# Attention and a squared-ReLU feed-forward on one core: the first batch's stores behind the third batch's transposes, and a smaller planned cost of exp

## The chip, the core and the metric

The kernel runs on one core of a Trainium2 chip. The metric is the time of one execution on the device in microseconds (us). Of the kernel before, four runs are given: median 421.77 us, from 421.56 to 421.96.

## What is computed

Grouped-query attention of 8 batches (16 query heads, 4 key and value heads, 384 positions, head size 64), followed by a feed-forward on the 3072 tokens:

```python
scores = q @ k.T / sqrt(64)            # each key head serves 4 query heads
attn   = exp(scores) / sum(exp(scores))
x      = (attn @ v)                     # heads side by side: [3072, 1024]
h      = maximum(x @ w_in, 0)           # [3072, 2048]
out    = (h * h) @ w_out                # [3072, 1024]
```

The reference subtracts the row's maximum before exp; the kernel does without, since the scores are small. Inputs and output are float32; the kernel multiplies in bf16 and adds up in float32.

## The kernel before, in words

**Stages.** The work goes by batch. For a batch b, SyncE's DMA transposes bring keys and queries into the layouts `kT` and `qT` (`turn_k_dma`, L277; `turn_q_dma`, L283, in two halves of eight heads each). For batch 0 and part of batch 1, TensorE transposes instead (L296, L313). Then:

- scores: `burst_small`, TensorE L339, writes pieces of two PSUM banks each, a total of 512 columns in each bank; ScalarE takes exp of a piece in one instruction (L349) into `expT`. Pieces alternate between banks 0, 1 and banks 2, 3, so that a piece needs the exp of the piece but one before it to be done. A batch has 18 pieces; the first half of the queries serves the first nine.
- values: `av`, TensorE L365, 8 steps of 18 matmuls in each batch; VectorE takes reciprocals of the row sums (L374) and multiplies (L380) into `o_sb`, which frees the bank of the step. SyncE transposes `o_sb` into `xT` (L385).
- feed-forward up: TensorE L460 in quads of four tiles (`quad`). A quad is 64 matmuls on half of the rows of the array each, in eight parts of eight, in banks 4 to 7; VectorE applies the maximum with zero (L473) and squares (L480, some on ScalarE, L477) into `h2T`. A batch has four quads; batch 0 computes four of its tiles with whole rows, early (L423).
- feed-forward down: TensorE L522, VectorE copies the sum to `y_sb` (L531), SyncE stores it (L534). There are six such copies and stores in a batch, and six halves of `y_sb`.

**What lies beside what.** The scores of batch b + 1 are issued between the quads of batch b, so that ScalarE's exp runs beside TensorE's feed-forward. The stretch with scores and quads is called split in the code. When it is over, the values of batch b + 1 follow, then the down products of batch b. GpSimd issues the loads of q, k and v two batches ahead and of both weight matrices, copies keys twice side by side (`dup_k`, L268), and copies values (`aug_v`, L273).

**What sets the order.** Each engine runs its own instructions in the order in which they are recorded (`Recorder.add`); semaphores carry the dependencies. The order comes from a planner, the loop from L666. It keeps a modelled clock for each engine (`R.clock`), advanced by the `cost` of each recorded operation, and models the time at which an operation's inputs and banks are free (`R.when`). At each turn it lists candidates (turn, values, scores "sc", feed-forward "ffn", ...) with their times, and takes the one of best priority among those that are ready. So a cost moves no work by itself; it decides in which order instructions stand on TensorE, and which wait comes with them. Two rules matter here. For the scores, L721 sets the time:

```python
t = max(R.when(reads=reads) + 3.0 * (b == 2 and not split), R.when(writes=[...]))
```

and for opening a split stretch, L735 and L736 ask for batches from 2 on that the planned time of the transposed queries lies within 6 us.

**Chores.** `prepare(b)` (L625) queues five steps: `dup_k`, the key transpose, the two halves of the query transpose, `aug_v`. Each is issued by the planner at L688 when its input is planned to be there. Stores are recorded at once, in `down_part`, when the last of the four parts of a down product is recorded. When all chores of a batch are issued, `turned` takes that batch's number.

Of the kernel before, what the change touches and what calls it, by code (L numbers as in the profile page):

```python
# [141 lines left out]
def bass_gqa_attention__then__ffn_squared_relu_kernel(  # L142
# [24 lines left out]
    R = Recorder(nc)  # L167
# [26 lines left out]
    def bank(i):  # L194
        return ps[:, i, :]
# [4 lines left out]
    def pick(allowed):  # L200
        turn_count[0] += 1
        i = min(allowed, key=lambda i: (max(R.when(writes=[("bank", i)]), R.clock["tensor"]), used[i]))
        used[i] = turn_count[0]
        return i
# [119 lines left out]
    def score_reads(b, u, c0=0, n=HC):  # L324
        g = u // NJ
        return [("kT", b % 2, g)] + [("qT", b % 2, g, t) for t in range(c0 // 128, (c0 + n) // 128)]

    def q_cols(b, g, x, c0, c1):
        flat = qT[b % 2][64 * x:64 * x + 64, 6 * g:6 * g + 6, :].rearrange("p n c -> p (n c)")
        return flat[:, c0:c1]  # L330

    def burst_small(b, pieces, base):

        n, c0, wide = (b * NU + pieces[0][0]) % NEX, pieces[0][1], pieces[0][2]

        def sc(pe):
            for m, (u, _, _) in enumerate(pieces):
                for x in range(2):
                    mm = pe.matmul(ps[:, base + x, m * wide:(m + 1) * wide],  # L339
                                   kT[b % 2][64 * x:64 * x + 64, u, :], q_cols(b, u // NJ, x, c0, c0 + wide))  # L340
            return mm

        total = wide * len(pieces)
        keys = [("bank", base), ("bank", base + 1)]
        R.add("tensor", sc, reads=[r for p in pieces for r in score_reads(b, *p)], writes=keys,
              cost=total / 2400 + (0.01 if b else 0.2))
        src = ps[:, base:base + 2, 0:total].rearrange("p x (k c) -> p x k c", k=len(pieces))
        dst = expT[:, n:n + len(pieces), :, c0:c0 + wide].rearrange("p k x c -> p x k c")
        R.add("scalar", lambda e: e.activation(dst, src, AF.Exp, scale=0.125), reads=keys,  # L349
              writes=[("expT", (b * NU + u) % NEX, t) for u, _, _ in pieces  # L350
                      for t in range(c0 // 128, (c0 + wide) // 128)], cost=(0.3 if b else 0.07) + total / 600)

    def av_reads(b, c):
        return [("expT", (b * NU + c // 2 * NJ + j) % NEX, 3 * (c % 2) + t) for j in range(NJ) for t in range(3)] + [("v_aug", b % 2), ("v_one", b % 2)]
# [138 lines left out]
    def downs(b):  # L493

        items = []
        for jj in range(2 if b == 0 else 0):
            ats = [[] for _ in range(NJ)]
            for tiles in ((0, 1), (2,)):
                for half in range(2):
                    for i3 in tiles:  # L500
                        for part in (2 * half, 2 * half + 1):
                            items.append(down_part(b, jj, i3, 512 * jj, 512 * jj + 512, part, ats[i3]))
        for jj in range(2 if b else 0):
            for i3 in range(NJ):
                last = b == B - 1 and (jj, i3) == (1, NJ - 1)
                for c0, c1 in ((512, 896), (896, 1024)) if last else ((512 * jj, 512 * jj + 512),):
                    at = []
                    for part in range(4):
                        items.append(down_part(b, jj, i3, c0, c1, part, at))
        return items  # L510

    def down_part(b, jj, i3, c0, c1, part, at):
        n = c1 - c0

        def piece():
            if part == 0:
                at.append(pick((6, 7)))
            i = at[0]

            def mm(pe):  # L520
                for c in range(4 * part, 4 * part + 4):
                    m = pe.matmul(bank(i)[:, 0:n], h2T[:, c, i3 * 128:(i3 + 1) * 128],  # L522
                                  w_out_sb[:, c, c0:c1], start=(c == 0), stop=(c == NFC - 1))
                return m

            R.add("tensor", mm, reads=need, writes=[("bank", i)], cost=4 * (n / 2400 + 0.0025))
            if part == 3:
                yb = y_n[0] % (2 * NY)
                y_n[0] += 1
                ysl = y_sb[yb // 2][:, (yb % 2) * 512:(yb % 2) * 512 + n]  # L530
                R.add("vector", lambda e: e.tensor_copy(ysl, bank(i)[:, 0:n]),  # L531
                      reads=[("bank", i)], writes=[("y", yb)], cost=0.08 + n / 960)
                rows = out[b * S:(b + 1) * S, :].rearrange("(p j) f -> j p f", j=NJ)[i3]
                R.add("sync", lambda e: e.dma_start(rows[:, c0:c1], ysl),  # L534
                      reads=[("y", yb)], writes=[("out", b, i3, c0)], dma=f"y{yb}", cost=0.6)
                stored.append(("out", b, i3, c0))

        need = [("w_out", jj, part // 2)] + [("h2T", c) for c in range(4 * part, 4 * part + 4)]
        return 0, need, (6, 7) if part == 0 else None, piece

    stored = []


    ones = nc.const_aps.tensor(1.0, (128, 128), bf16)
# [5 lines left out]
        out=ident[:], in_=ident[:], compare_op=ALU.not_equal, fill=1.0, base=0,  # L550
# [26 lines left out]
    def warm_up(n, cost):  # L577
        def body(pe):
# [8 lines left out]
          reads=[("k_f32", 0)], writes=[("k_dup", 0, 0, 0)], cost=0.27)  # L587
    R.add("scalar", lambda e: e.copy(k_dup[0][:, 0:NJ, 1, :], k_f32[:, 0:NJ, :]),
          reads=[("k_f32", 0)], writes=[("k_dup", 0, 0, 1)], cost=0.27)
# [3 lines left out]
          reads=[("q_f32", 0)], writes=["q_lead"], cost=0.3)  # L593
    for n in range(2):
        a, z = 384 * n + 192 * (n == 0), 384 * n + 384
        R.add("scalar", lambda e, a=a, z=z: e.copy(q_to[:, a:z], q_from[:, a:z]),
              reads=[("q_f32", n)], writes=[("q_st", 0, 0, n)], cost=0.35 + 0.15 * n)
# [17 lines left out]
    sc_q = [(b, n) for b in range(B) for n in range(len(later if b else smalls))]  # L615
# [3 lines left out]
    scored, pairs, turned = set(), 0, 1  # L619
# [13 lines left out]
    def open_bank(banks):  # L633
        return min(R.when(writes=[("bank", i)]) for i in banks)
# [3 lines left out]
    def ff_head(split):  # L638

        if ff["now"]:  # L640
            return ff["now"][0]
        n = 4 if split else 1
        if ff["tiles"]:
            if len(ff["tiles"]) < n:
                return None
            return (quad(ff["b"], ff["tiles"][:4]) if split else up_tile(ff["b"], ff["tiles"][0]))[0]
        return ff["down"][0] if ff["down"] and not split else None
# [14 lines left out]
    split = False  # L662
# [3 lines left out]
    while av_q or av_open or sc_q or o_q or lanes or ff["now"] or ff["tiles"] or ff["down"]:  # L666
        now = R.clock["tensor"]
# [20 lines left out]
        while chores and R.when(reads=chores[0][0], eng="none") <= now + margin:  # L688
            chores.pop(0)[1]()
            if not chores:  # L690
                turned = queued
        cand = []
        wait = 0.1 if split else 0.0
        if turn_q:
            b, g, w = turn_q[0]
# [5 lines left out]
        elif av_q:  # L701
            b, c = av_q[0]
# [6 lines left out]
        if sc_q:  # L709
            b, u = sc_q[0]  # L710
            pieces = (later if b else smalls)[u]
            tiles = {(b, x, t) for x, c0, n in pieces for t in range(c0 // 128, (c0 + n) // 128)}
            ok = {(b, x // NJ, t) for _, x, t in tiles} <= turned_g if b < 2 else turned >= b
            ok = ok and pairs // 2 * NJ + NEX > b * NU + max(x for _, x, _ in tiles)
            if b and not split:
                ok = ok and at_edge and (u > 0 or pairs >= 8 * b and ff["b"] == b - 1 and len(ff["tiles"]) >= 4)
            if ok:
                reads = [r for p in pieces for r in score_reads(b, *p)]
                if b and not split:
                    reads += [("xT", (b - 1) % NXT, kc) for kc in range(NKC)]  # L720
                t = max(R.when(reads=reads) + 3.0 * (b == 2 and not split), R.when(writes=[("bank", 2 * (u % 2) + i) for i in range(2)]))  # L721
                cand.append((t, 0, "sc"))
        early_banks[:] = [i for i in ((6, 7, 0, 1, 2, 3) if sc_q and sc_q[0] == (1, 0) else (6, 7)) if i not in held]
        for n, lane in enumerate(lanes):
            chunks, need, banks, _ = lane[0]
            if x_done[0] >= chunks:
                t = R.when(reads=need)
                if banks is not None:
                    if not banks:
                        continue  # L730
                    t = max(t, open_bank(banks))
                cand.append((t, 5 + 0.1 * n, n))
        opening = (not split and at_edge and bool(sc_q) and sc_q[0][1] == 0 and sc_q[0][0] == ff["b"] + 1
                   and pairs >= 8 * sc_q[0][0] and len(ff["tiles"]) >= 4)
        if opening and sc_q[0][0] > 1:  # L735
            opening = R.when(reads=score_reads(sc_q[0][0], 0)) < now + 6.0  # L736
        f_head = ff_head(split or opening) if not lanes else None
        if f_head is not None:
            chunks, need, banks, piece = f_head
            if x_done[ff["b"]] >= chunks:  # L740
                t = R.when(reads=need)
                if banks:
                    t = max(t, max(open_bank([i]) for i in banks) if split or opening else open_bank(banks))
                cand.append((t, 5, "ffn"))
        if split and at_edge and len(ff["tiles"]) < 4 and not (sc_q and sc_q[0][1]):
            split = False
# [6 lines left out]
        if not cand:  # L753
            chores.pop(0)[1]()
            if not chores:
                turned = queued
# [6 lines left out]
        if split and what[2] not in ("sc", "ffn"):  # L763
            split = False
        if what[2] == "turn":
            b, g, w = turn_q.pop(0)
# [5 lines left out]
        elif what[2] == "av":  # L772
            b, c = av_q.pop(0)
            av_open = (b, c, av(b, c, spare))
            next(av_open[2])
        elif what[2] == "av2":
            b, c, rest = av_open
# [8 lines left out]
        elif what[2] == "o":  # L786
            b, c, _ = o_q.pop(0)
            turn_o_pe(b, c, spare)
            x_done[b] += 1
        elif what[2] == "sc":  # L790
            b, u = sc_q.pop(0)
            if b and not split:
                split = True
# [6 lines left out]
        else:  # L800
            if opening:
                split = True
# [32 lines left out]
```

## Time and profile before

| | |
|---|---|
| median of four runs | 421.77 us |
| profiled execution | 421.86 us |
| its span in the profile | 419.8 us |
| TensorE busy | 414.1 us of the span, 99% |
| VectorE, ScalarE, GpSimd busy | 199.9, 154.0, 55.3 us |
| L522 matmuls (down), 784 | 168.2 us busy |
| L460 matmuls (up), 1728 | 159.7 us busy |
| L349 exp, 146 | 138.1 us busy, mean 1017 ns |
| granted TensorE clock | full speed in all of the span |

The span is the part of the profiled execution that the profile shows; the execution is 2.1 us longer. Busy times of TensorE's rows overlap within the pipeline, so that rates are better read from the distance between starts than from the mean of one. PE is TensorE's matmuls, PEld its weight loads, DVE VectorE, ACT ScalarE, POOL GpSimd, SP SyncE; a q after the name is the engine's queue of issued DMAs. An arrow in brackets gives the idle time before a row and what ended it. L-numbers are lines of the kernel.

### The profile page before, as it was taken

What the parts mean: (1) busy time and instruction counts of PE and PEld (TensorE: products, weight loads), DVE (VectorE), ACT (ScalarE), POOL (GpSimd) and SP (SyncE); (2) the same over time, 40 slices, a digit from 0 to 9 for tenths busy, and PEclk for the clock granted to TensorE, in tenths of its full rate; (3) what the DMA queues carried; (4) which work ended last, traced back from release to release, by engine and by line L of the source; (5) the groups of instructions that cost most, each with busy time, mean ns of one, the idle gap of its engine ahead of it and who ended that gap; (6) DMA issues with size and microseconds to landing.
All of it is one profiled execution on the core that took longest, in us unless ns stands there. A gap on an engine that the chain in (4) does not pass through costs nothing.

```text
span 419.8 us, 9623 instructions
## 1 busy us (share of the span) xinstructions
PE 414.1 (99%) x4328; PEld 236.4 (56%) x4328; DVE 199.9 (48%) x434; ACT 154.0 (37%) x176; POOL 55.3 (13%) x68
## 2 busy tenths in 40 slices
PE   8999999999999999999999999999999999999997
PEld 5566744467445674465645566455744567446544
DVE  3664751358424683146811667225851458324312
ACT  6958600285008700286004840058200780004300
POOL 8680010143203000400012000000000000000000
PEclk9999999999999999999999999999999999999999
DMA  9999999999999019920499004810052001420012
GB/s 180 193 174 200 206 187 176 245 127 124 175 230 139 2 26 161 221 48 2 53 214 183 5 2 84 206 52 2 3 125 77 27 2 20 115 79 15 0 74 78
DMA packets 96921, 44.40 MB, mean 106 GB/s; under 512 B 77296, under 2 KB 90864, under 8 KB 96880
## 3 DMA queue, kind: packets, MB, share of 16 engines
q0 software_dynamic: 36544, 17.44, 32.7%
q1 hardware_dynamic: 59664, 25.86, 28.6%
q8 instruction: 34, 0.56, 0.6%
q10 hardware_dynamic: 672, 0.49, 0.4%
q14 instruction: 7, 0.06, 0.0%
HBM read 35.65 MB, written 12.58 MB: 115 GB/s over the span
## 4 chain that ended last, share of the span: by engine, by line
PE 92%; DMA 3%; DVE 2%; ACT 1%; POOL 1%; issue 0%; SPq 0%; POOLq 0%
PE ps L522 39%; PE ps L460 32%; PE ps L339 7%; PE ps L365 7%; PE ps L423 6%; DMA qT<-q_st 2%; DMA q_st<-in_q_dram 1%; DVE h2T L480 1%; ACT expT L349 1%; DVE hr L473 0%; PE ps L313 0%; SPq L534 0%; PE ps L398 0%; DVE o_sb L380 0%; DVE y_sb L531 0%
## 5 line engine op out<-in xcount | busy, mean ns | idle before, releaser
L349 ACT ACTIVATE expT<-ps 128x1024 bf16<-128x1024 f32 (+1 forms) x146 | 138.1, 1017 | 150.4 <-PE ps L339 150.3
L522 PE MATMUL ps<-w_out_sb,h2T 128*128 128x512 bf16 (+2 forms) x784 | 168.2, 375 | 0.0
L460 PE MATMUL ps<-xT,w_in_sb 64*128 64x384 bf16 x1728 | 159.7, 323 | 0.0
L522 PEld LDWEIGHTS ps<-w_out_sb,h2T 128*128 128x128 bf16 x784 | 75.2, 98 | 86.6
L460 PEld LDWEIGHTS ps<-xT,w_in_sb 64*128 64x128 bf16 x1728 | 83.9, 94 | 56.9 <-issue 0.4
L473 DVE TENSOR_SCALAR hr<-ps 128x384 f32<-128x384 f32 x108 | 55.2, 552 | 78.3 <-PE ps L460 78.3
L531 DVE COPY y_sb<-ps 128x512 f32<-128x512 f32 (+2 forms) x49 | 33.3, 680 | 113.2 <-PE ps L522 113.2
L339 PE MATMUL ps<-qT,kT 64*128 64x256 bf16 (+2 forms) x384 | 54.0, 324 | 1.6 <-DMA qT<-q_st 0.9
L480 DVE TENSOR_TENSOR h2T<-hr 128x384 bf16<-128x384 f32 x102 | 51.1, 561 | 0.0
L365 PEld LDWEIGHTS ps<-v_aug,expT 128*128 128x128 bf16 x1152 | 37.1, 98 | 6.2 <-issue 1.3
L365 PE MATMUL ps<-v_aug,expT 128*128 128x65 bf16 x1152 | 39.7, 193 | 0.3 <-issue 0.2
L380 DVE TENSOR_TENSOR o_sb<-ps,rinv 128x384 bf16<-128x384 f32 x64 | 35.7, 557 | 2.2
L423 PE MATMUL ps<-xT,w_in_sb 128*128 128x384 bf16 x160 | 27.3, 326 | 0.0
L339 PEld LDWEIGHTS ps<-qT,kT 64*128 64x128 bf16 x384 | 17.7, 94 | 16.8 <-issue 2.4
L433 ACT ACTIVATE h2T<-hr 128x384 bf16<-128x384 f32 x20 | 10.4, 523 | 44.1 <-DVE hr L431 44.0
L273 POOL COPY v_aug<-v_st 128x768 bf16<-128x768 bf16 x8 | 6.7, 836 | 126.6 <-PE ps L365 88.7
L423 PEld LDWEIGHTS ps<-xT,w_in_sb 128*128 128x128 bf16 x160 | 15.4, 98 | 9.8 <-issue 0.2
L477 ACT ACTIVATE h2T<-hr 128x384 bf16<-128x384 f32 x6 | 3.1, 523 | 46.6 <-DVE hr L473 46.6
L431 DVE TENSOR_SCALAR hr<-ps 128x384 f32<-128x384 f32 x20 | 11.0, 556 | 12.6 <-PE ps L423 12.5
L241 POOL DMA_DIRECT2D q_st<-in_q_dram x17 | 14.8, 885 | 0.9 <-POOLq L820 0.8
L374 DVE RECIPROCAL rinv<-ps 128x6 f32<-128x6 f32 x64 | 11.9, 186 | 4.0 <-PE ps L365 4.0
L268 POOL COPY k_dup<-k_st 128x1536 bf16<-128x1536 bf16 x7 | 10.3, 1467 | 26.1 <-DMA k_st<-in_k_dram 26.1
(28 smaller groups left out, 58.4 us busy)
## 6 DMA issues: line engine op xcount, KB each, us to landing
out_dram<-y_sb SPq DMA_DIRECT2D x47, 256.0 KB, 2.8
q_st<-in_q_dram POOLq DMA_DIRECT2D x14, 384.0 KB, 8.2
w_in_sb<-in_moe_w_in_dram POOLq DMA_DIRECT2D x8, 512.0 KB, 15.3
w_out_sb<-in_moe_w_out_dram POOLq DMA_DIRECT2D x4, 1024.0 KB, 28.6
v_st<-in_v_dram POOLq DMA_DIRECT2D x8, 192.0 KB, 10.0
k_st<-in_k_dram POOLq DMA_DIRECT2D x7, 192.0 KB, 3.9
q_st<-in_q_dram POOLq DMA_DIRECT2D x3, 192.0 KB, 5.3
xT<-o_sb SPq DMA_TRANSPOSE x28, 2.8
```

What stands on the lines that cost most here:

```text
L241: R.add("gpsimd", lambda g: g.dma_start(q_st[st][:, h0:h1, :], q[b, h0:h1].rearrange("h (p j) d -> p h (j d)", j=NJ)), writes=[("q_st", st ...
L339: mm = pe.matmul(ps[:, base + x, m * wide:(m + 1) * wide], kT[b % 2][64 * x:64 * x + 64, u, :], q_cols(b, u // NJ, x, c0, c0 + wide))
L349: R.add("scalar", lambda e: e.activation(dst, src, AF.Exp, scale=0.125), reads=keys, writes=[("expT", (b * NU + u) % NEX, t) for u, _, _ i ...
L365: m = pe.matmul(po[:, f - 6 * s2, 0:D + 1], w, v_aug[b % 2][:, g * NJ + j, 0:D + 1], start=(j == 0), stop=(j == NJ - 1))
L374: R.add("vector", lambda e: e.reciprocal(rinv[r].ap().unsqueeze(2), po[:, :, D:D + 1]), reads=[("bank", i)], writes=[("rinv", r)], cost=0.22)
L380: R.add("vector", lambda e: e.tensor_tensor(dst, srcv, rbv, ALU.mult), reads=[("bank", i), ("rinv", r)], writes=[("o_sb", o, s2)], cost=0.48)
L423: m = pe.matmul(bank(i)[:, 0:S], w_in_sb[:, kc, c * 128:(c + 1) * 128], xT[b % NXT][:, kc, :], start=(kc == 0), stop=(kc == NKC - 1))
L460: m = pe.matmul(bank(4 + xs[x])[:, 0:S], w_in_sb[r, kc, c * 128:(c + 1) * 128], xT[b % NXT][r, kc, :], start=(phase < 2 and kc == 0), stop ...
L473: R.add("vector", lambda e, r=r, i=i: e.tensor_scalar_max(hr[r][:, :], bank(4 + i)[:, 0:S], 0.0), reads=[("bank", 4 + i)], writes=[("hr", ...
L480: hr_read[r] = (R.add("vector", lambda e, c=c, r=r: e.tensor_tensor(h2T[:, c, :], hr[r][:, :], hr[r][:, :], ALU.mult), reads=[("hr", r)], ...
L522: m = pe.matmul(bank(i)[:, 0:n], h2T[:, c, i3 * 128:(i3 + 1) * 128], w_out_sb[:, c, c0:c1], start=(c == 0), stop=(c == NFC - 1))
L531: R.add("vector", lambda e: e.tensor_copy(ysl, bank(i)[:, 0:n]), reads=[("bank", i)], writes=[("y", yb)], cost=0.08 + n / 960)
```

## The change

Three parts. The six stores of batch 0 are no longer recorded when their down product is; a function that records them is kept in a list, and the list is emptied at the planner's first turn at which `turned` is over 1, that is, when the transposes of batch 2 (the third batch) have all been issued. The copies to `y_sb` stay where they are. The planned cost of exp for batches from 1 on goes from 0.3 to 0.2 us plus the same share for its columns. And two rules on the start of scores are altered: the 3.0 us by which batch 2's first score was planned later become 1.5 us for its first nine pieces, and the rule at L735 is removed.

```diff
-              writes=[...], cost=(0.3 if b else 0.07) + total / 600)
+              writes=[...], cost=(0.2 if b else 0.07) + total / 600)
...
-                R.add("sync", lambda e: e.dma_start(rows[:, c0:c1], ysl),
-                      reads=[("y", yb)], writes=[("out", b, i3, c0)], dma=f"y{yb}", cost=0.6)
+                put = lambda: R.add("sync", lambda e: e.dma_start(rows[:, c0:c1], ysl),
+                                    reads=[("y", yb)], writes=[("out", b, i3, c0)], dma=f"y{yb}", cost=0.6)
                 stored.append(("out", b, i3, c0))
+                if b:
+                    put()
+                else:
+                    held_back.append(put)
...
-    stored = []
+    stored, held_back = [], []
...
+        while turned > 1 and held_back:
+            held_back.pop(0)()
...
-                t = max(R.when(reads=reads) + 3.0 * (b == 2 and not split), R.when(writes=[...]))
+                t = max(R.when(reads=reads) + 1.5 * (b == 2 and u < 9), R.when(writes=[...]))
...
-        if opening and sc_q[0][0] > 1:
-            opening = R.when(reads=score_reads(sc_q[0][0], 0)) < now + 6.0
```

More of the change, by code (lines that the diff above doesn't have):

```diff
@@ L350, in burst_small @@
               writes=[("expT", (b * NU + u) % NEX, t) for u, _, _ in pieces
-                      for t in range(c0 // 128, (c0 + wide) // 128)], cost=(0.3 if b else 0.07) + total / 600)
+                      for t in range(c0 // 128, (c0 + wide) // 128)], cost=(0.2 if b else 0.07) + total / 600)
     def av_reads(b, c):
@@ L720, in bass_gqa_attention__then__ffn_squared_relu_kernel @@
                     reads += [("xT", (b - 1) % NXT, kc) for kc in range(NKC)]
-                t = max(R.when(reads=reads) + 3.0 * (b == 2 and not split), R.when(writes=[("bank", 2 * (u % 2) + i) for i in range(2)]))
+                t = max(R.when(reads=reads) + 1.5 * (b == 2 and u < 9), R.when(writes=[("bank", 2 * (u % 2) + i) for i in range(2)]))
                 cand.append((t, 0, "sc"))
```

## The prediction

> **What bounds the kernel now.** I read the page's parts 1 and 4 first, then the chain of waits around the only place where a DMA stands on it, then SyncE's queue there, and last TensorE's own timeline at the ends of the score stretches. Part 1:
>
> ```profile
> span 419.8 us, 9623 instructions
> PE 414.1 (99%) x4328; PEld 236.4 (56%) x4328; DVE 199.9 (48%) x434; ACT 154.0 (37%) x176; POOL 55.3 (13%) x68
> ```
>
> TensorE is the bound; at 99% an edit can only win back the few places where it stands still. Those are to be found, not averaged. Past the first 30 us the list of waits names one of PE's on another engine or queue: L339 (scores) on the transposed queries. The chain there (start, length, what):
>
> ```profile
> 71.07 0.70 DVE y_sb L531
> ...
> 72.86 0.54 SPq L534
> 73.40 0.04 issue
> 73.44 7.89 DMA qT<-q_st
> 81.33 0.05 issue
> 81.38 0.60 PE ps L339 x4
> ```
>
> The first scores of batch 2 wait for a transpose that was issued only after five output stores, the fifth of which waited for VectorE's copy at 71.07. SyncE's queue in that stretch says the same:
>
> ```profile
> 65.37 5.36 SPq L277 DMA_TRANSPOSE kT<-k_dup  x1
> 70.77 2.63 SPq L534 DMA_DIRECT2D out_dram<-y_sb  x5
> 73.44 3.14 SPq L283 DMA_TRANSPOSE qT<-q_st  x1
> ```
>
> How much it costs, from TensorE's rows:
>
> ```profile
> 74.41 6.02 PE L460 MATMUL ps<-xT,w_in_sb 64*128 64x384 bf16 x72
> 81.38 0.60 PE L339 MATMUL ps<-qT,kT 64*128 64x512 bf16 x4 [0.94 <-DMA qT<-q_st]
> 81.82 1.46 PE L460 MATMUL ps<-xT,w_in_sb 64*128 64x384 bf16 x16
> 83.12 0.38 PE L339 MATMUL ps<-qT,kT 64*128 64x256 bf16 x4
> ```
>
> Sixteen L460 matmuls take 83.12 - 81.82 = 1.30 us start to start, 0.0813 each. The 72 from 74.41 are over at 74.41 + 5.85 = 80.26; the scores start at 81.38: 1.12 us lost (the 0.94 shown leaves out the pipeline's tail).
>
> A second loss is hidden in the value products (L365), whose first 126 run in one piece:
>
> ```profile
> 48.62 4.26 PE L365 MATMUL ps<-v_aug,expT 128*128 128x65 bf16 x126
> 52.72 1.03 PE L522 MATMUL ps<-w_out_sb,h2T 128*128 128x512 bf16 x4
> ...
> 100.33 4.26 PE L365 MATMUL ps<-v_aug,expT 128*128 128x65 bf16 x126
> 104.43 1.03 PE L522 MATMUL ps<-w_out_sb,h2T 128*128 128x512 bf16 x4
> ...
> 150.60 4.01 PE L365 MATMUL ps<-v_aug,expT 128*128 128x65 bf16 x126
> 154.44 1.03 PE L522 MATMUL ps<-w_out_sb,h2T 128*128 128x512 bf16 x4
> ```
>
> In batch 3 (and alike in 4 to 7) they take 154.44 - 150.60 = 3.84 us, 30.5 ns each. In batches 1 and 2 they take 4.10: 0.26 lost each. The weight loads say why:
>
> ```profile
> 103.26 0.56 DVE L380 TENSOR_TENSOR o_sb<-ps,rinv 128x384 bf16<-128x384 f32 x1
> 103.87 0.60 PEld L365 LDWEIGHTS ps<-v_aug,expT 128*128 128x128 bf16 x18 [0.20 <-DVE o_sb L380]
> ```
>
> The seventh group of 18 needs a bank that VectorE frees at 103.82. Batch 1 loses a further 54.46 - 53.58 = 0.88 against 0.55 in its eighth group: 0.33, marked "issue", with no releaser.
>
> [...] The trace agrees: it moves 410, 397 and 385 GB/s from 75 to 78 us, a rate seen at none of the loads or transposes around it, while the query transpose, issued since 73.44, lands only at 81.33. [...] from 78 to 79 us, when the half is under way, the windows show 284 GB/s in all. [...] L480 is one: 1.18 us at its longest between 88 and 97 us, when GpSimd copies run, against a median of 0.55.
>
> **The change, part by part.** What moves is read from the listing of both kernels' instructions by engine. VectorE, ScalarE and GpSimd have the same instructions in the same order; only SyncE's and TensorE's orders differ.
>
> (1) *Stores held back.* On SyncE the two query transposes follow the key transpose directly, and the six stores of batch 0 come after. The first half is then issued at 70.77, when the key transpose's issue ends. [...] The half is 128 x 12 x 128 x 2 B = 393 KB[...]. Bound above: the longest issue to landing here, 7.89, gives 70.77 + 7.89 = 78.66. When is it wanted? TensorE's order now has 64 L460 matmuls ahead of the scores, not 72: 74.41 + 64 x 0.0813 = 79.61. Both ends are earlier, so the stall goes: -1.12. The second half [...] is wanted nine score pieces on, which is over 8 us.
>
> The moved stores: six issues of 0.5 us each behind the second half's issue (about 77 us), landing 5.3 later by their median, so near 86. Who waits? The next writer of these y_sb halves is VectorE's first copy of batch 1 at 108.63: 20 us of cover. No other SyncE work is passed: the next key transpose waits for GpSimd's copy of 87.40 anyway. [...] I take zero.
>
> (2) *Shorter exp, and the start offsets.* The planner's exp falls from 0.3 + 512/600 to 0.2 + 512/600, 1.15 to 1.05 us. In batches 3 to 7 the last score moves forward: 88 L460 matmuls follow it, not 64. Between first and last piece lie 256 - 88 = 168 of them, 13.7 us, and 18 pieces of 0.217, 3.9 us: 17 steps of 1.03 us. An exp in a row of four advances by (3.77 - 1.02) / 3 = 0.92, so the banks still come free in time: following the order piece by piece with these durations, the least slack before a piece is 0.20 us, and it is 0.20 in the old order too. Work is only exchanged: zero, on 99% of the span. The 24 + 64 in a row cross a boundary between quads with no score to cover VectorE's clearing; the 72 at 74.41 already do that and run 6.02 - 5.85 = 0.17 over, which is the last matmul's tail. Zero again.
>
> (3) *Ends of the stretches of batches 1 and 2.* There the order becomes 108 value products, four L522, 36 value products. Six groups need six banks; the four L522 (0.87 us) now stand before the seventh group. In batch 2 that group comes at 100.33 + 3.29 + 0.87 = 104.5 and its bank, with VectorE's last quad ending 0.22 later (the score no longer follows it), at 104.04; the eighth at 105.04, bank at 104.73. So -0.26, and in batch 1 alike. Bound on the other side for batch 2: GpSimd's key copy of 104.95 comes up to 5 us sooner and may lie beside L480 at 101.2, adding 0.6 as shown; then the eighth group waits for 105.3, +0.3 instead. Batch 1 has no such copy moved.
>
> (4) The check removed from `opening` shows nothing of its own in the order: zero. The 0.33 "issue" of batch 1 has no cause in the trace; between -0.33 and 0. I take 0.
>
> Sum: -1.12 - 0.26 - 0.26 = -1.64. The profiled execution took 421.86 (span 419.8 and 2.1 around it): 420.22. It stands 0.09 above the median of 421.77; on that, 420.13. I say 420.2.
>
> **The rivals.**
> A. *Value products still wait* in one or both batches, because GpSimd slows VectorE or the banks are picked otherwise. For: VectorE's chain has only 0.3 us of slack at the eighth group. Against: the L522 stand between. 421.77 - 1.12 = 420.65, up to 420.9 with the loss of 0.3.
> B. *The query transpose is late anyway*, since the loads on GpSimd's queue share the engines until about 74. A landing after 79.56 costs us for us; at 80.7 the gain of (1) is gone: 421.77 - 0.52 = 421.25. For: the keys took 10.0. Against: both ends above.
> C. *ScalarE becomes the bound* of the score stretch: slower. It decides from an exp period of 1.03 us; were it the 1.05 that the planner uses plus 0.07 for the signal, 1.12, then 17 x 0.09 = 1.5 us per stretch, six or seven stretches, about 10 us: 430. At 1.05 alone, 7 x 17 x 0.02 = 2.4 us: 422.5. Against: 0.92 measured.
>
> **Numbers.** Forecast 0.62, A 0.20, B 0.12, C 0.06. About 0.2%, 0.84 us, is what can be told from no change, so the line for faster is 420.93: forecast and A are faster, 0.82; B the same, 0.12; C slower, 0.06. Range: down to 421.77 - 1.64 - 0.33 = 419.8; up past A's end to 421.0. Outside are B and C, 0.18.
>
> **What would show it.** Right: no PE wait of L339 on qT near 79.6; the half landing before 79; the stores issued after both halves; 108 value products taking 3.3 us and no VectorE wait in the 36; the steps from batch 3 on still 50.0 us. Wrong: L339 waiting for ScalarE's exp in the stretches (C), for qT (B), or L365 for o_sb (A).

## The result, and the profile after

The changed kernel takes 420.83 us (median of 38 runs, 419.45 to 422.54); the kernel before takes 422.06 beside it (59 runs, 421.39 to 424.14). The ratio is 0.9965 [0.9957, 0.9972]. The profiled execution of after took 420.75 us, 1.11 less than that of before. The forecast was 420.2, with a range of 419.8 to 421.0: the time lies in the range and is faster. The totals don't settle by how much. The medians differ by 1.23 us and the ratio stands for 1.2 to 1.8, which takes in the forecast's 1.64; the time itself, 420.83, is where rival A stood (420.65 to 420.9), but before took 0.29 more here than the 421.77 from which both were reckoned. The traces tell the two apart.

The head of the page, and SyncE's queue around the transposes of batch 2 (start, length, what):

```profile
span 418.7 us, 9624 instructions
...
PE 413.6 (99%) x4328; PEld 235.3 (56%) x4328; DVE 200.5 (48%) x434; ACT 151.9 (36%) x176; POOL 55.4 (13%) x68
```
```profile
65.39 5.36 SPq L277 DMA_TRANSPOSE kT<-k_dup  x1
70.80 5.09 SPq L283 DMA_TRANSPOSE qT<-q_st  x2
75.94 4.29 SPq L534 DMA_DIRECT2D out_dram<-y_sb  x6
```

The two query transposes now follow the key transpose at once, and the stores come behind. On TensorE the scores of batch 2 start without a wait:

```profile
73.66 5.37 PE L460 MATMUL ps<-xT,w_in_sb 64*128 64x384 bf16 x64
78.87 0.59 PE L339 MATMUL ps<-qT,kT 64*128 64x512 bf16 x4
```

From 73.66 to 78.87 are 5.21 us for 64 matmuls, 0.0814 each: nothing is lost. Before, 6.97 us passed for 72 that take 5.85, which is the 1.12 of step (1).

Now the value products at the ends of the stretches of batches 1, 2 and 3:

```profile
48.45 3.46 PE L365 MATMUL ps<-v_aug,expT 128*128 128x65 bf16 x108
51.75 1.03 PE L522 MATMUL ps<-w_out_sb,h2T 128*128 128x512 bf16 x4
52.62 1.26 PE L365 MATMUL ps<-v_aug,expT 128*128 128x65 bf16 x36
53.71 2.54 PE L522 MATMUL ps<-w_out_sb,h2T 128*128 128x512 bf16 x11
...
98.47 3.46 PE L365 MATMUL ps<-v_aug,expT 128*128 128x65 bf16 x108
101.76 1.02 PE L522 MATMUL ps<-w_out_sb,h2T 128*128 128x512 bf16 x4
103.49 1.41 PE L365 MATMUL ps<-v_aug,expT 128*128 128x65 bf16 x36 [0.71 <-DVE o_sb L380]
104.74 1.46 PE L522 MATMUL ps<-w_out_sb,h2T 128*128 128x512 bf16 x6
...
149.50 4.01 PE L365 MATMUL ps<-v_aug,expT 128*128 128x65 bf16 x126
...
154.76 1.46 PE L522 MATMUL ps<-w_out_sb,h2T 128*128 128x512 bf16 x6
```

Measure the whole group, 144 value products and four L522, from its first row to the next L522. In batch 3 it is 154.76 - 149.50 = 5.26 us, and nothing waits in it. Batch 1 now takes 53.71 - 48.45 = 5.26 as well (before 5.84). Batch 2 takes 104.74 - 98.47 = 6.27 (before 5.51): it has become *worse* by 0.76, and the row of 36 names VectorE. Why VectorE is late there is read from its own rows and GpSimd's, first before, then after:

```profile
101.16 1.95 DVE L480 TENSOR_TENSOR h2T<-hr 128x384 bf16<-128x384 f32 x4
...
104.95 1.47 POOL L268 COPY k_dup<-k_st 128x1536 bf16<-128x1536 bf16 x1 [0.35 <-DMA k_st<-in_k_dram]
```
```profile
99.52 3.22 DVE L480 TENSOR_TENSOR h2T<-hr 128x384 bf16<-128x384 f32 x4
...
102.88 0.56 DVE L380 TENSOR_TENSOR o_sb<-ps,rinv 128x384 bf16<-128x384 f32 x1
...
100.23 1.63 POOL L268 COPY k_dup<-k_st 128x1536 bf16<-128x1536 bf16 x1 [0.79 <-DMA k_st<-in_k_dram]
```

The key copy of batch 4, which began at 104.95 before, begins at 100.23, in the middle of VectorE's last four squares. Those take 3.22 us; the four of before took 1.95. The lengths of the four (ns, least/median/most):

```profile
L480 DVE TENSOR_TENSOR h2T<-hr x4: 544/551/1817, 99.5 to 102.2; 128x384 bf16<-128x384 f32 x4
```

Three of them are untouched and one takes 1817 ns, 1.27 us more, and the first bank of batch 2's values comes free that much later.

**Where the time went**, from the same points in both profiles (start of the value products, us):

| | batch 1 | batch 2 | batch 3 | batch 1 to 3 |
|---|---|---|---|---|
| before | 48.62 | 100.33 | 150.60 | 101.98 |
| after | 48.45 | 98.47 | 149.50 | 101.05 |

The opening gave -1.12, the values of batch 1 -0.58, those of batch 2 +0.76: together -0.94, against 101.05 - 101.98 = -0.93. From batch 3 on nothing differs (starts at 199.51, 249.53, 299.54 and 349.56, steps of 50.02). The remaining -0.17 (48.45 - 48.62) is the start of the kernel, which varies: a second profile of after has 48.75, and over all the kernels below, some of which order batch 1 differently, batch 1's values begin anywhere from 48.37 to 50.06. So the stretch from batch 1 to batch 3 is the cleaner measure, and each experiment is given with it.

### The profile page after: what moved, and what is told of

Same layout as the page of the kernel before. It is cut to its first block, busy times and chain, and to the rows that moved or that the text cites. A ratio compares the mean times of both kernels' runs of the same rounds, so it can differ in the third digit from the quotient of the medians.

```text
span 418.7 us, 9624 instructions
## 1 busy us (share of the span) xinstructions
PE 413.6 (99%) x4328; PEld 235.3 (56%) x4328; DVE 200.5 (48%) x434; ACT 151.9 (36%) x176; POOL 55.4 (13%) x68
## 4 chain that ended last, share of the span: by engine, by line
PE 95%; DVE 1%; DMA 1%; ACT 1%; POOL 1%; issue 0%; POOLq 0%
PE ps L522 39%; PE ps L460 34%; PE ps L365 8%; PE ps L339 8%; PE ps L423 6%; DMA q_st<-in_q_dram 1%; DVE h2T L480 1%; ACT expT L349 1%; PE ps L313 0%; PE ps L398 0%; DVE hr L473 0%; PE ps L296 0%; POOL q_st L241 0%; POOL v_st L234 0%; DVE o_sb L380 0%
## 5 line engine op out<-in xcount | busy, mean ns | idle before, releaser
L349 ACT ACTIVATE expT<-ps 128x1024 bf16<-128x1024 f32 (+1 forms) x146 | 136.1, 1021 | 141.3 <-PE ps L339 141.2
L522 PE MATMUL ps<-w_out_sb,h2T 128*128 128x512 bf16 (+2 forms) x784 | 168.2, 375 | 0.0
L522 PEld LDWEIGHTS ps<-w_out_sb,h2T 128*128 128x128 bf16 x784 | 75.2, 98 | 86.5
L480 DVE TENSOR_TENSOR h2T<-hr 128x384 bf16<-128x384 f32 x102 | 51.7, 566 | 0.0
L365 PEld LDWEIGHTS ps<-v_aug,expT 128*128 128x128 bf16 x1152 | 36.9, 97 | 6.8 <-DVE o_sb L380 1.4
L365 PE MATMUL ps<-v_aug,expT 128*128 128x65 bf16 x1152 | 39.3, 193 | 0.7 <-DVE o_sb L380 0.7
L380 DVE TENSOR_TENSOR o_sb<-ps,rinv 128x384 bf16<-128x384 f32 x64 | 35.7, 557 | 2.2
```

The lines of the kernel that those rows point to most:

```text
L365: m = pe.matmul(po[:, f - 6 * s2, 0:D + 1], w, v_aug[b % 2][:, g * NJ + j, 0:D + 1], start=(j == 0), stop=(j == NJ - 1))
L380: R.add("vector", lambda e: e.tensor_tensor(dst, srcv, rbv, ALU.mult), reads=[("bank", i), ("rinv", r)], writes=[("o_sb", o, s2)], cost=0.48)
L480: hr_read[r] = (R.add("vector", lambda e, c=c, r=r: e.tensor_tensor(h2T[:, c, :], hr[r][:, :], hr[r][:, :], ALU.mult), reads=[("hr", r)], ...
```

## The experiments

The theory after these two profiles: the opening was won, and most of what the values should have added is lost again because earlier transposes bring GpSimd's copy onto VectorE's squares. The rivals: the copy is innocent and VectorE is late for another reason; or the gain comes from the pacing and not from the stores.

| kernel | median us | ratio to before | batch 1 to 3 |
|---|---|---|---|
| after | 420.83 | 0.9965 [0.9957, 0.9972] | 101.05 |
| stores held back only | 421.15 | 0.9978 [0.997, 0.9986] | 101.26 |
| pacing only | 420.33 | 0.9963 [0.995, 0.9976] | 100.24 |
| after, copy later | 420.41 | 0.9963 [0.9952, 0.9974] | 100.23 |
| after, copy on ScalarE | 420.15 | 0.9954 [0.9942, 0.9966] | 100.03 |
| stores only, copy on ScalarE | 420.54 | 0.9961 [0.995, 0.9973] | 100.43 |
| before, planned exp 0.2 only | 423.53 | 1.0039 [1.0027, 1.005] | 103.10 |
| after, copy on ScalarE, exp 0.1 | 419.50 | 0.9941 [0.9929, 0.9953] | 100.05 |
| after, copy on ScalarE, exp 0.0 | 423.49 | 1.0031 [1.0019, 1.0043] | 101.09 |
| after once more | 421.09 | 0.9969 [0.9956, 0.9981] | 101.09 |
| before, first stores on ScalarE's queue | 426.55 | 1.011 [1.0094, 1.0126] | 107.17 |

**1. Each half alone.** First the held-back stores with the old planned cost and the old rules (against after):

```diff
-              writes=[...], cost=(0.2 if b else 0.07) + total / 600)
+              writes=[...], cost=(0.3 if b else 0.07) + total / 600)
...
-                t = max(R.when(reads=reads) + 1.5 * (b == 2 and u < 9), R.when(writes=[...]))
+                t = max(R.when(reads=reads) + 3.0 * (b == 2 and not split), R.when(writes=[...]))
...
+        if opening and sc_q[0][0] > 1:
+            opening = R.when(reads=score_reads(sc_q[0][0], 0)) < now + 6.0
```

> The changed kernel with the old exp cost (0.3) and both old rules on the start of scores; only the stores of batch 0 are held back. On TensorE the scores of batch 2 stand behind 64 up matmuls, and batch 2 ends in 126 value products in one piece. Theory (the held-back stores win 1.1 us at the opening, but GpSimd's key copy comes forward onto VectorE's last quad and the value products of batch 2 pay for it): no L339 wait on qT near 79; the four L480 at batch 2's end take about 3.2 us and not 1.95; the seventh group of value products, with no L522 before it, waits 1.2 to 1.6 us. Net about 0: 421.8 to 422.3, ratio to before 0.999 to 1.001. Rival (the pacing is what brings the collision, the stores alone keep their gain): about 421.0, ratio 0.9974.

Measured: 0.9978 [0.997, 0.9986], just below the theory's 0.999 and with the rival's 0.9974 inside the interval. The theory had the loss too large, and one of its reasons was wrong: batch 2 does not end with 126 value products in one piece here, the planner puts 108, the L522 and then 36. TensorE's, VectorE's and GpSimd's rows:

```profile
74.43 5.38 PE L460 MATMUL ps<-xT,w_in_sb 64*128 64x384 bf16 x64
79.64 0.60 PE L339 MATMUL ps<-qT,kT 64*128 64x512 bf16 x4
...
104.05 1.42 PE L365 MATMUL ps<-v_aug,expT 128*128 128x65 bf16 x36 [0.49 <-DVE o_sb L380]
...
100.07 3.22 DVE L480 TENSOR_TENSOR h2T<-hr 128x384 bf16<-128x384 f32 x4
...
100.67 1.74 POOL L268 COPY k_dup<-k_st 128x1536 bf16<-128x1536 bf16 x1 [0.29 <-DMA k_st<-in_k_dram]
```

The opening is free of waits (79.64 - 74.43 = 5.21) and the same 3.22 us stand beside the copy. So both the gain and the loss belong to the held-back stores, 1.12 against 0.81 (99.24 to 150.06 is 50.82 from batch 2 to 3, where 50.01 is free of waits): less than the whole gain, so that something is left. What the pacing adds in after is batch 1: from its values to those of batch 2 are 99.24 - 48.80 = 50.44 us here and 98.47 - 48.45 = 50.02 in after.

Then the pacing alone, with the stores issued at once:

```diff
-                if b:
+                if True:
                     put()
```

> The changed kernel with the stores of batch 0 recorded at once, as before; exp cost 0.2 and the new rules stay. The planner now puts 96 up matmuls ahead of batch 2's first scores: they are wanted at 74.4 + 7.8 = 82.2, after the landing at 81.3 seen before. Theory (TensorE's order, not the transposes' place, decides the opening; and with late transposes GpSimd's copy stays behind batch 2's values): no qT wait, no wait of 0.2 or more at the value products of batches 1 and 2: 1.1 + 0.26 + 0.26 = 1.6 us saved, 420.4, ratio 0.9962, better than the whole change. Rival (holding back the stores is needed for the 1.1): a qT wait of about 1 us stays near 82, and 421.5, ratio 0.9988.

Measured: 0.9963, as the theory had it, and the same as after. TensorE, SyncE's queue and the copy:

```profile
73.81 7.97 PE L460 MATMUL ps<-xT,w_in_sb 64*128 64x384 bf16 x96
81.62 0.60 PE L339 MATMUL ps<-qT,kT 64*128 64x512 bf16 x4
...
70.73 2.65 SPq L534 DMA_DIRECT2D out_dram<-y_sb  x5
73.43 2.73 SPq L283 DMA_TRANSPOSE qT<-q_st  x1
...
104.40 1.47 POOL L268 COPY k_dup<-k_st 128x1536 bf16<-128x1536 bf16 x1 [0.34 <-DMA k_st<-in_k_dram]
```

The query transpose is as late as before (issued at 73.43), and yet nobody waits: the planner has put 96 feed-forward matmuls ahead of the scores, not 64. The copy stays behind the squares. So there are two ways to the same 1.1 us, an earlier transpose or more work in front of it, and only the first brings the copy onto the last squares of a stretch. In the totals this kernel can't be told from after, but its stretch from batch 1 to 3 is 0.81 shorter: without the held-back stores the rest of the change does at least as well. Nor is a stall of VectorE a loss by itself. Here the copy of batch 3, at 87.11, holds a square just as long:

```profile
86.23 3.22 DVE L480 TENSOR_TENSOR h2T<-hr 128x384 bf16<-128x384 f32 x4
```

TensorE's list of waits shows none for it. In the middle of this stretch there is slack; at the end of batch 2's, where the values need the banks that VectorE frees, there is not enough.

**2. Is it the copy?** Three kernels take it away from the squares. In the first it is made to wait for the last value of batch 2, in the second ScalarE does it (both against after), and in the third ScalarE does it in the kernel with the stores alone:

```diff
-              reads=[("k_st", b % NST) if b else ("k_f32", g) for g in range(g0, g1)],
+              reads=[("k_st", b % NST) if b else ("k_f32", g) for g in range(g0, g1)] + [("o_sb", 11 % NO, 1)] * (b == 4),
```
```diff
-        R.add("gpsimd", lambda e: e.tensor_copy(dst, src),
+        R.add("scalar" if b == 4 else "gpsimd", lambda e: e.copy(dst, src) if b == 4 else e.tensor_copy(dst, src),
```

> The changed kernel, with one more dependency: GpSimd's key copy of batch 4 waits for VectorE's last multiplication of batch 2's values, so that it runs some 6 us later, behind them. Theory (that copy[...] stretches L480 and so delays the banks): L480 x4 at batch 2's end back to 1.95 us, no wait before the 36 value products, 1.0 us less than the changed kernel: about 419.8, ratio to before 0.9948. Rival (L480 is slowed by the DMA traffic of the loads and transposes there, or the wait has another cause): unchanged, 420.8, ratio 0.997.

> The changed kernel, with the same key copy of batch 4 done by ScalarE, as soon as the keys have landed, at about 100 us, beside the same L480. Theory [...]: L480 x4 takes 1.95 us although a copy runs beside it; 1.0 us less than the changed kernel, ratio to before 0.9948, as with the late copy. Rival (any copy of that size into SBUF slows VectorE): L480 x4 over 2.5 us, ratio about 0.997.

> Only the stores of batch 0 are held back (old exp cost, old rules), and the key copy of batch 4 is done by ScalarE, so that it doesn't run beside VectorE's L480 on GpSimd. Theory (the stores alone win the opening's 1.1 us, and the first run with them lost about 0.6 of it to the copy): no wait on qT, batch 2's value products without a wait (they stand as 108, four L522, 36 here too), batch 1's wait of about 0.25 still there since its 126 stand in one piece. 1.1 + 0.25 = 1.35 us under before: about 420.7, ratio 0.9968. Rival (the copy was not what cost the first run its gain): 421.15, ratio 0.9978, as without this edit.

Measured: 0.9963, 0.9954 and 0.9961. The totals don't settle it: the second and third hold the theory's number in their intervals, the first holds the rival's, and all three overlap with after's. The rows do. The sharpest is the third, since it has the same copy at nearly the same time as the stores alone (100.67), only on another engine:

```profile
100.01 1.96 DVE L480 TENSOR_TENSOR h2T<-hr 128x384 bf16<-128x384 f32 x4
...
100.21 1.46 ACT L268 COPY k_dup<-k_st 128x1536 bf16<-128x1536 bf16 x1
```

The copy lies wholly inside the squares, moves the same bytes between the same tiles, and the squares take 1.96 instead of 3.22. The stretch from batch 2 to 3 falls from 50.82 (stores only) to 50.01; in after it falls from 51.03 to 50.01 with the copy later or on ScalarE. So it is neither the traffic of the copy nor VectorE's own load: it is that GpSimd does it. With the copy on ScalarE, the stretch from batch 1 to 3 is 100.03, which is 1.95 under before: 1.12 + 0.26 + 0.26 of the forecast, and the 0.33 of batch 1 that the forecast left out (sum 1.97).

Part of why these 1.0 us aren't seen in full in the totals is the start again: the profiled executions of after and of the copy on ScalarE have spans of 418.7 and 418.2, but the second begins batch 1's values 0.48 later (48.93 against 48.45).

**3. How far the planned exp can go.** Before with the new planned cost and nothing else:

```diff
-              writes=[...], cost=(0.3 if b else 0.07) + total / 600)
+              writes=[...], cost=(0.2 if b else 0.07) + total / 600)
```

> The kernel before with the exp cost 0.2 and nothing else. The planner then opens batch 2's stretch with 8 whole-row up matmuls and 64 of a quad, and finds no quad for the end of it: six score pieces stand almost without feed-forward between them. Theory (the shorter cost needs the other parts of the change): a qT wait of 0.3 to 0.5 stays, ScalarE's exp holds the last pieces back for about 1.2 us, 0.5 won at the value products; net 421.8 to 422.4, ratio 0.999 to 1.001. Rival (the shorter cost is the part that wins): about 420.9, ratio 0.997.

Measured: 1.0039, slower by more than was expected.

```profile
73.83 1.46 PE L423 MATMUL ps<-xT,w_in_sb 128*128 128x384 bf16 x8
75.22 5.37 PE L460 MATMUL ps<-xT,w_in_sb 64*128 64x384 bf16 x64
81.50 0.61 PE L339 MATMUL ps<-qT,kT 64*128 64x512 bf16 x4 [0.90 <-DMA qT<-q_st]
...
97.75 0.39 PE L339 MATMUL ps<-qT,kT 64*128 64x512 bf16 x2 [0.91 <-ACT expT L349]
98.58 0.72 PE L365 MATMUL ps<-v_aug,expT 128*128 128x65 bf16 x18 [0.44 <-DVE o_sb L380]
```

The opening still waits for the late transpose, though eight whole-row matmuls were put ahead of it, and the scores, now spread into the values of batch 2, wait for ScalarE and for VectorE's banks. Batch 1 to 3 takes 103.10, 1.12 more than before. So the shorter cost alone is no gain; the pacing kernel, which has the new rules on the start of the scores as well, is one. No run has the rules without the cost, so that what the cost adds to them stays open.

Then after, with the copy on ScalarE, at 0.1 and at 0.0 instead of 0.2. Rival C asked when ScalarE becomes the bound, and 0.0 was chosen to cross that line, since it plans 512/600 = 0.853 us for an exp:

```diff
-              writes=[...], cost=(0.2 if b else 0.07) + total / 600)
+              writes=[...], cost=(0.1 if b else 0.07) + total / 600)
```

> The changed kernel with the key copy of batch 4 on ScalarE and a planned exp cost of 0.1 + columns/600 (0.95 us), between the change's 0.2 and the 0.0 tried before. Theory (ScalarE bounds a stretch only where the planned step is under the exp's real advance of 0.90 us): no piece waits for an exp; as with 0.2, ratio 0.9954, 420.1. Rival (every shortening of the cost brings waits): about half of the 3 us that 0.0 cost, ratio 0.999.

> The changed kernel with the key copy of batch 4 on ScalarE, and the planned exp cost at 0.0 + columns/600 (0.85 us) where the change has 0.2. The planner now puts eight up matmuls between all score pieces: a step of 0.865 us where an exp advances by 0.903. Theory (ScalarE becomes the bound of a stretch once the step falls under the exp's advance): TensorE waits 0.03 to 0.04 us for an exp at about ten pieces of each stretch, 0.3 us a stretch, 2.2 us in all; 422.3, ratio 1.0005. Rival (the slack of two pairs of banks is enough for 18 pieces): as the run with the copy on ScalarE, 420.15, ratio 0.9954.

Measured: 0.9941 at 0.1, lower than either expected, and 1.0031 at 0.0, higher than either. At 0.1 the stretch from batch 1 to 3 is 100.05, as with 0.2 (100.03), and no score waits. The lower median is therefore not explained by the pieces; its interval overlaps with that of 0.2, and I claim no gain from it. Its profiled execution, at 421.18 the slowest of its six, shows what the start can cost, in the list of waits past 30 us:

```profile
PE ps L460 <- DMA w_in_sb<-in_moe_w_in_dram: 1.2, 1, 1.2
```

At 0.0 the pieces on TensorE stand 135.06 - 134.14 = 0.92 us apart, and ScalarE's row shows 14 exps without a pause:

```profile
129.37 12.97 ACT L349 ACTIVATE expT<-ps 128x1024 bf16<-128x1024 f32 x14
...
134.14 0.39 PE L339 MATMUL ps<-qT,kT 64*128 64x512 bf16 x2
...
135.06 0.39 PE L339 MATMUL ps<-qT,kT 64*128 64x256 bf16 x4
```

An exp advances by (12.97 - 1.02) / 13 = 0.92. The planner's order asks for one every 0.87 (a piece's 0.217 and eight matmuls of 0.0813), so each piece in such a run is late by some 0.05, and a batch takes 50.55 us instead of 50.02. ScalarE is the bound there, at 0.92 against a plan of 0.853; with a plan of 0.953 it is not. (In both kernels the planner also gives ScalarE more of the squares, 12 and 13 of them against 6, but none stands among these 14.) Rival C's mechanism exists, and the change stays on the safe side of it.

**4. The loss again.** After, unchanged, beside the others:

> The changed kernel as it is, on the chip and beside the runs of before that the others of this call share. Both theories: ratio 0.9965, about 420.8; wait of about 0.9 us before the 36 value products of batch 2, L480 x4 about 3.2 us beside GpSimd's copy. If the copy theory is right it is about 0.6 to 1.0 us over the kernels whose copy was moved.

Measured: 0.9969. Another execution of it shows the same stall, to the hundredth:

```profile
99.85 3.22 DVE L480 TENSOR_TENSOR h2T<-hr 128x384 bf16<-128x384 f32 x4
```

**5. Another way to take the stores out of the queue.** Before, with the stores of batch 0 issued by ScalarE:

```diff
-                R.add("sync", lambda e: e.dma_start(rows[:, c0:c1], ysl),
+                R.add("sync" if b else "scalar", lambda e: e.dma_start(rows[:, c0:c1], ysl),
```

> The kernel before, but the six stores of batch 0 are issued by ScalarE, which has nothing to do from 50 to 78 us[...]. SyncE issues the query transposes directly after the keys', and 64 up matmuls stand ahead of batch 2's scores, which are wanted at about 79.6. Theory (the transposes were late because the stores stood ahead of them in SyncE's queue[...]): the first half lands by about 79.5, no wait for qT or one under 0.4 us; GpSimd's copy comes forward as with the stores held back: ratio about 0.998. Rival (the stores' 1.3 MB share the DMA engines[...]): landing near 81 or later, a wait of 1 to 2 us, ratio 1.000 to 1.003.

Measured: 1.011, 4.7 us slower than the 421.83 of before beside it. The theory missed and the rival was too mild. SyncE's and ScalarE's queues, then TensorE:

```profile
67.01 7.00 SPq L277 DMA_TRANSPOSE kT<-k_dup  x1
74.06 8.62 SPq L283 DMA_TRANSPOSE qT<-q_st  x2
...
61.18 14.18 ACTq L534 DMA_DIRECT2D out_dram<-y_sb  x5
...
83.44 0.61 PE L339 MATMUL ps<-qT,kT 64*128 64x512 bf16 x4 [3.66 <-DMA qT<-q_st]
```

ScalarE issues the stores from 59.45 on, beside the transposes. The key transpose begins at 67.01, 1.6 later than before, and its issue takes 7.00 us instead of 5.36, so the query transpose starts at 74.06, 3.3 later than in after and even later than before (73.44); its first half lands 9.3 us after its issue, not 7.9. The key transpose lands 12.7 us after its issue, not 10.0. So a queue of its own didn't keep the stores out of the transposes' way: *later* was the cure here and *elsewhere* was not. How stores slow a transpose on another queue, no run shows. The stall at the end of batch 2 is there too: the value products (L365) wait 0.5 us for VectorE's `o_sb` in the list of waits past 30 us, with four squares of 3.22 us from 105.56 and GpSimd's copy at 106.43 beside them, and 155.54 - 104.72 = 50.82 us from batch 2 to 3. After the wait of 3.66 us TensorE is slow as well (us, then busy time of each engine, PEclk, DMA share, GB/s):

```profile
84.00:86.00 2.00, 2.00 (x19) 0.95 (x15) 0.00 (x0) 1.81 (x2) 0.83 (x2) 0.58 0.10 20
86.00:88.00 2.00, 2.00 (x18) 1.11 (x16) 0.00 (x0) 1.02 (x1) 2.00 (x3) 0.56 0.66 70
```

## The prediction, point by point

**The bound** was read rightly: TensorE at 99% before and after, and only its few stops moved the time.

**(1) Stores held back**: right, -1.12 as said, but on thinner ice than its working showed. The first half was issued at 70.80 (said 70.77) and landed 7.6 us later, at 78.40; the step rests on its outer bound of 78.66, which held. The scores wanted it at 78.87, so that 0.5 us were left, where the bound left 0.95 (79.61 - 78.66). From 74 to 76 us 264 and 274 GB/s were moved, near the 284 read in before, but then came a hole. After, and below it the same hole before:

```profile
75.00:76.00 1.00, 1.00 (x16) 0.61 (x14) 0.00 (x0) 0.00 (x0) 0.02 (x1) 1.00 1.22 274
76.00:77.00 1.00, 1.00 (x16) 0.61 (x14) 0.00 (x0) 0.00 (x0) 0.00 (x0) 1.00 2.35 136
77.00:78.00 1.00, 1.00 (x16) 0.61 (x14) 0.22 (x1) 0.00 (x0) 0.00 (x0) 1.00 0.06 7
78.00:79.00 1.00, 1.00 (x16) 0.58 (x12) 0.80 (x2) 0.52 (x1) 0.00 (x0) 1.00 1.13 254
```
```profile
79.00:80.00 1.00, 1.00 (x16) 0.53 (x14) 0.72 (x3) 0.52 (x1) 0.00 (x0) 1.00 2.16 63
```

Rival B was half a microsecond from coming true. The line of before was on hand, and the prediction laid the lateness on the stores alone: in before the rate stays under 15 GB/s from 79.25 to 80.5, which is as long as the stall of 1.12. The five stores ahead of the first half there, issued from 70.77 to 72.86, landed 5.2 to 5.8 us later, by 78.7 at the latest, and the half at 81.33; that they held it back by more than the order of issue was the author's estimate. Taking the stores away was enough; whether taking the hole away would have been enough as well, no run shows. The moved stores cost nothing, as said: they are issued from 75.94 to 80.23 and TensorE's list of waits past 30 us names only VectorE's banks.

**(2) Shorter exp**: right. Steps of 50.02 us from batch 3 on, no score waits for ScalarE; the two kernels at 0.1 and 0.0 bracket the place where it would. The step of 1.03 counts a piece too many: 17 pieces lie between the first start and the last, which makes 1.02, and the trace has (142.03 - 124.69) / 17 = 1.02. Nothing hangs on it.

**(3) Ends of the stretches**: right in batch 1 (its bank wait is gone), wrong in batch 2. The forecast was -0.26 there, with +0.3 as the bound on the other side; measured is +0.76. This is the step that failed: the collision of GpSimd's copy with VectorE's squares was taken not to happen and, as a bound, was priced at half of what it cost. The danger was named, "GpSimd's key copy of 104.95 comes up to 5 us sooner and may lie beside L480", and the copy did come 4.72 sooner (the 5 were an estimate of the author's). Two choices in the working were wrong. I took it not to collide, though 104.95 less "up to 5" reaches 99.95, and the squares, from 101.2 in before and 1.4 sooner by the terms ahead of them, were to be expected from 99.8 to about 101.8: the overlap was likelier than not. And I priced it from the slowest square seen, as +0.6. The slowest square in before, 1.18, had met only the values' copy, of 0.89 us; the key copy is 1.47 long. What I didn't see is that before holds a meeting with a key copy as well:

```profile
87.40 1.47 POOL L268 COPY k_dup<-k_st 128x1536 bf16<-128x1536 bf16 x1 [0.50 <-DMA k_st<-in_k_dram]
...
88.16 1.58 DVE L480 TENSOR_TENSOR h2T<-hr 128x384 bf16<-128x384 f32 x2
```

The first of these two squares takes 1.11 us, so it ends at 89.27, 0.41 after the copy's end at 88.87 (by the unrounded times). This square began late in the copy, 0.76 after its start, so its stall was short, while its end still follows the copy's. After shows the same: the third square starts at 100.45, the copy ends at 100.23 + 1.63 = 101.86, the square at 100.45 + 1.82 = 102.27, 0.41 after it, about the 0.47 that a square advances when alone ((1.95 - 0.55) / 3 in before's four). In the kernel with the stores only the copy ends at 102.41 and the one long square, 1.82 from 101.00, at 102.82: again 0.41. Priced so, the stall is nearly the copy's length, 1.3 us instead of 0.6. With the slack of 0.3 at the eighth group that the prediction worked out, 1.0 is lost over the free run, and with the 0.26 of old loss gone the bound would have been +0.74; +0.76 came. The recorded +0.3 is itself a slip in the sum: 0.6 less the slack of 0.3 is what is lost over the free run, and against before, which had lost 0.26 there, only +0.04.

**(4) The 0.33 of batch 1** was taken as nothing, with -0.33 as a bound. In after it is gone (5.84 to 5.26 is 0.26 + 0.32), but in other kernels a gap of 0.14 to 0.32 shows up again at the same place, in the one with ScalarE's queue too. No run shows its cause; that stays open.

**The sum.** Forecast -1.12 - 0.26 - 0.26 = -1.64; measured -1.12 - 0.58 + 0.76 = -0.94, with -0.17 from the start of the kernel. Rival A, "GpSimd slows VectorE", is what happened in one of its two batches, with 420.65 to 420.9 as its time. That the total still lies in the range is in part luck: the loss in batch 2 was 1.02 worse than forecast, and the 0.32 of batch 1, taken as nothing and still unexplained, came off on the other side. Without it the time would have been about 421.15 (an estimate, 420.83 + 0.32), above the range.

## What to carry to other kernels

A transfer that comes sooner can bring what waits for it sooner, on engines that nobody looked at (here GpSimd's copy, by 4.72 us): follow it to the next instruction on each engine, and ask what will then run beside what. Price a collision by the time at which the instruction that holds the other one will end (here the square ended 0.41 us after the copy), not by the largest slowdown seen so far, and look whether it falls where the bound engine has slack. And when the effect is some tenths of a per cent, compare the distance between two fixed points inside the trace as well as the total, because the executions of after alone lay 3 us apart (419.45 to 422.54), more than the effect.

## What the runs showed of the hardware

- One GpSimd copy of 128x1536 bf16 (1.47 us alone) held one VectorE multiplication of 128x384 with two SBUF inputs for 1.27 us, 1817 ns instead of 550; the neighbours kept their 550. The same copy on ScalarE (1.46 us) held none.
- A held square's end follows the copy's end, not its own start. Past the first 30 us of the profiles of before and after four squares were lengthened beside a GpSimd copy, to 1053, 1110, 1176 and 1817 ns, and every one ended 0.41 us after the copy's end. The value multiplications (L380), which take one input from PSUM, met such copies 21 times there and kept their 556 to 558 ns.
- While a query transpose was under way in after, the transfers all but stopped for over a microsecond: 7 GB/s from 77 to 78 us, between 274 (75 to 76) and 254 GB/s (78 to 79). In the packets one of 16 KB, of the kind that the profile calls instruction, stands at the hole, from 76.38 to 77.30 in after and from 78.74 to 79.77 in before. But one from 88.83 to 89.81 in after has no hole beside it (192 GB/s). The cause stays open; no run took this packet away.
- Stores on a second engine's queue stretched a transpose's issue from 5.36 to 7.00 us and its way to landing from 10.0 to 12.7; TensorE's wait for the queries went from 0.94 to 3.66.
- After that wait the granted clock is 0.58 from 84 to 86 us and 0.56 from 86 to 88, and 16 up matmuls took 86.00 - 83.88 = 2.12 us instead of 1.30. From 70 to 84 it is 1.00, and the mean over the span, 0.996, leaves about 1.7 us of 424.8, which these two stretches make up (0.42 x 2 + 0.44 x 2 = 1.72). In the other eleven profiles the mean is 1.00; in the eight of them with a list of TensorE's waits past the first 30 us, the longest is 1.2 us. That the length of the wait decides it is not shown by one case.
